# Moving two rsqrts and one DMA transpose in the opening of a two-layer attention and MLP kernel

## The chip, the cores and the metric

The kernel runs on one core of one Trainium2 chip. The metric is the device time of one execution in microseconds. The median before was 1292.16 us over three runs (1291.91 to 1292.77).

## The reference, cut to what matters

```python
x = A_x                                             # 1 x 2048 x 1024, bf16
x = x + A(layernorm(x), A_wqkv, A_wo)               # local dilated attention, 32 heads
x = x + B(layernorm(x), B_w1, B_b1, B_w2, B_b2)     # layernorm again, then a token-mixing MLP
# ... and the same two lines once more
```

Only the opening of the first attention concerns this study: load x, normalise each token, transpose it, and multiply by the V part of `A_wqkv`.

## The kernel before: the parts that the change touches

Tokens are cut into 16 tiles of 128. For each tile k the opening does this:

- SyncE (SP) loads the tile from memory (`x_load`, 256 KB).
- VectorE (DVE) forms mean and variance (`S_` twice, then `A_`).
- ScalarE (ACT) computes `R_`, the inverse root, as a Ln and an Exp of one column.
- DVE normalises the tile in place (`N_`).
- SP issues a DMA transpose into `hT` (`T_`).
- TensorE (PE) runs 16 matmuls (`V_`, 8 chunks of depth by 2 halves of the width).
- ACT evacuates the PSUM result to SBUF (`E_`), which frees its PSUM buffer.

Tiles 0 to 2 are transposed on PE instead (tiles 0 and 1 once more by DMA later, after their normalisation): PE's first V matmul starts at 6.54 us, while the first DMA transpose is issued at 14.73 us. Each engine executes its own list in order (tile 7's Ln starts at 26.13 us, behind ACT's evacuation of tile 4, though its variance was ready at 23.77 us):

```python
act = [ ..., (E_, 1), (R_, 6), (E_, 2), (E_, 3)]
rs = [(R_, k) for k in range(7, NT)]
for k in range(4, NT):            # E_4, R_7, R_8, E_5, R_9, R_10, ...
    act.append((E_, k))
    act += rs[:2]
    del rs[:2]
# dve, for each k: ..., S_(k+1, 0), N_(k), S_(k+1, 1), A_(k+1), ...
sp = [ ..., (x_load, 10), (x_load, 11), (T_, 6), (x_load, 12), (x_load, 13), (x_load, 14),
      (x_load, 15), (T_, 7), (T_, 8), (T_, 9), (T_, 0), (T_, 1), *((T_, k) for k in range(10, NT)), ...]
# V_ writes the single PSUM buffer "acc" where k % 3 == 1 (tiles 1, 4, 7, 10, 13), else one of two "s" buffers,
# so V of 6 needs the evacuation of 3, and V of 7 that of 4.
```

The softmax here doesn't subtract the row's maximum and nothing guards it: scores larger than these inputs give would overflow.

## Time and profile before

| what | value | view |
|---|---|---|
| span | 1289.9 us | page |
| PE busy | 1285.3 us | page, engines |
| PE's longest wait after its start | 0.55 us, before tile 7's V | waits of PE |
| first QK matmul | 63.73 us | timeline of PE |

The chain that ended last, from 25.2 us in the kernel before. The columns are start in us, duration in us, and what it was. L278 is the evacuation, L178 and L179 the two halves of rsqrt, L192 the normalisation, L269 the V matmuls.

```profile
25.22 1.01 ACT v L278
26.23 0.20 ACT ln L178
26.43 0.02 issue
26.46 0.21 ACT rs L179
26.67 0.03 issue
26.69 0.55 DVE x L192
27.24 0.03 DVE bn L227
27.27 5.33 DMA hT<-x
32.60 0.04 issue
32.64 3.63 PE acc L269 x16
36.27 6.91 PE s L269 x32
```

Between the first microseconds and the last instruction of the kernel, this is the only place where the chain leaves PE. Tile 7's rsqrt stands behind the evacuation of tile 4, which stands behind PE; then follow normalisation and a transpose of 5.33 us.

The timeline of PE in the same kernel. The columns are start, duration, engine, line, operation, operands, count, and the idle time just before with what ended it.

```profile
14.65 7.08 PE L269 MATMUL s<-wv,hT 128*128 128x512 bf16 x32
21.57 3.62 PE L269 MATMUL acc<-wv,hT 128*128 128x512 bf16 x16
25.02 7.07 PE L269 MATMUL s<-wv,hT 128*128 128x512 bf16 x32
32.64 3.63 PE L269 MATMUL acc<-wv,hT 128*128 128x512 bf16 x16 [0.55 <-DMA hT<-x]
36.11 7.07 PE L269 MATMUL s<-wv,hT 128*128 128x512 bf16 x32
...
63.73 0.59 PE L377 MATMUL m<-hT,wqk 128*128 128x512 bf16 x2
```

From the start of tile 2's V (14.65) to the first QK matmul (63.73) the stretch is 49.08 us. And two tiles on the `s` buffers take 6.90 to 6.92 us from start to start where nothing stalls (36.11 to 43.01 by the same view, 14.65 to 21.57), but 7.62 us where the wait lies (25.02 to 32.64), 0.71 us more than the middle of these. The idle time printed is 0.55 us. The difference of 0.16 us is an overlap that this trace shows between V groups wherever PE does not stall: the printed end of a group lies 0.16 to 0.17 us behind the start of the next (14.65 plus 7.08 is 21.73, the next starts at 21.57). Idle time counted from a printed end is short by that much here.

### The profile page before, as it was taken

How to read it: one execution, taken by the hardware profiler on the slowest of the kernel's cores; microseconds unless marked ns; L12 is line 12 of the kernel's file. 1: busy time of each engine (PE TensorE's matmuls, PEld its weight loads, DVE VectorE, ACT ScalarE, POOL GpSimd, SP SyncE). 2: the span in 40 equal slices, each digit the busy share in tenths (PEclk: the TensorE clock that was granted, in tenths of full speed). 3: DMA queues.
4: the chain of work that ended last, by engine and by line, in shares of the span. 5: the costliest groups of instructions: out<-in, count | busy, mean ns of one | idle time of the engine just before them, and what ended most of it. 6: DMA issues, size and time to landing. Idle time of an engine off the chain costs nothing.

```text
span 1289.9 us, 19532 instructions
## 1 busy us (share of the span) xinstructions
PE 1285.3 (100%) x8422; PEld 592.0 (46%) x8422; DVE 417.6 (32%) x855; ACT 369.2 (29%) x609; POOL 2.4 (0%) x15
## 2 busy tenths in 40 slices
PE   9999999999999999999999999999999999999999
PEld 4444444444444444444444444444444444444444
DVE  6566777820000022322300677688000000111111
ACT  4356664531111110000033666645311111000000
POOL 0000000000000000000000000000000000000000
PEclk9999999999999999999999999999999999999999
DMA  8711123642222144465510111247423222334330
GB/s 239 112 47 49 49 83 128 204 141 80 66 85 74 57 122 127 133 165 129 132 31 1 49 49 51 80 151 220 114 68 92 69 62 82 100 106 138 115 92 33
DMA packets 204102, 126.59 MB, mean 98 GB/s; under 512 B 44272, under 2 KB 183792, under 8 KB 204016
## 3 DMA queue, kind: packets, MB, share of 16 engines
q1 hardware_dynamic: 204016, 125.35, 34.6%
q8 instruction: 66, 1.08, 0.4%
q14 instruction: 20, 0.16, 0.0%
HBM read 96.48 MB, written 16.78 MB: 88 GB/s over the span
## 4 chain that ended last, share of the span: by engine, by line
PE 99%; DMA 1%; DVE 0%; ACT 0%; issue 0%
PE m L377 18%; PE s L619 15%; PE s L572 15%; PE m L492 9%; PE acc L619 7%; PE acc L572 7%; PE m L572 7%; PE m L619 7%; PE m L362 4%; PE s L269 2%; PE s L408 2%; PE acc L269 1%; PE acc L443 1%; PE acc L447 1%; DMA hT<-x 0%; DMA x<-in_A_x_dram 0%
## 5 line engine op out<-in xcount | busy, mean ns | idle before, releaser
L619 PEld LDWEIGHTS <-w 128*128 128x128 bf16 x1820 | 177.0, 98 | 210.1
L572 PEld LDWEIGHTS <-w 128*128 128x128 bf16 x1792 | 175.3, 98 | 211.5
L377 PE MATMUL m<-hT,wqk 128*128 128x512 bf16 x1024 | 231.7, 380 | 0.0
L572 PE MATMUL s<-h,w 128*128 128x512 bf16 x896 | 202.8, 379 | 0.0
L619 PE MATMUL s<-g,w 128*128 128x512 bf16 (+1 forms) x924 | 201.6, 374 | 0.0
L621 DVE SCALAR_TENSOR_TENSOR xo<-s,b_sb,xs 128x512 bf16<-128x512 f32 (+1 forms) x33 | 24.4, 739 | 532.9 <-PE s L619 530.8
L377 PEld LDWEIGHTS <-wqk 128*128 128x128 bf16 x1024 | 95.2, 98 | 118.0 <-issue 10.7
L423 DVE TENSOR_TENSOR Pm<-pc,band 32x640 bf16<-32x640 bf16 x256 | 123.6, 483 | 56.2 <-ACT pc L411 49.4
L492 PE MATMUL m<-wo,oT 128*128 128x512 bf16 x512 | 111.5, 379 | 0.0
L572 PE MATMUL acc<-h,w 128*128 128x512 bf16 x448 | 103.9, 379 | 0.0
L619 PE MATMUL acc<-g,w 128*128 128x512 bf16 x448 | 100.6, 379 | 0.0
L572 PE MATMUL m<-h,w 128*128 128x512 bf16 x448 | 99.0, 379 | 0.0
L619 PE MATMUL m<-g,w 128*128 128x512 bf16 (+1 forms) x448 | 97.8, 376 | 0.0
L178 ACT ACTIVATE ln<-mv,eps 128x1 f32<-128x1 f32 x64 | 18.8, 294 | 228.9 <-DVE mv L186 184.9
L492 PEld LDWEIGHTS <-oT 128*128 128x128 bf16 x512 | 49.6, 98 | 60.3 <-issue 1.3
L579 ACT ACTIVATE g<-s,b_sb 128x1024 bf16<-128x1024 f32 x28 | 31.2, 1114 | 158.2 <-PE s L572 158.2
L388 DVE COPY qB<-qs 32x512 bf16<-32x512 bf16 x136 | 38.2, 281 | 95.7 <-ACT qs L384 94.3
L362 PE MATMUL m<-wv,hT 128*128 128x512 bf16 x256 | 55.4, 379 | 0.0
L411 ACT ACTIVATE pc<-s,shift 128x640 bf16<-128x640 f32 x64 | 51.2, 800 | 11.7 <-PE s L408 11.7
L384 ACT CAST qs<-m 128x512 bf16<-128x512 f32 x64 | 37.5, 586 | 48.3 <-PE m L377 48.3
L381 ACT CAST kT<-m 128x512 bf16<-128x512 f32 x64 | 37.5, 586 | 46.4 <-PE m L377 46.4
L499 DVE TENSOR_TENSOR xn<-m,xr 128x512 bf16<-128x512 f32 x64 | 44.2, 690 | 16.9 <-PE m L492 16.8
(67 smaller groups left out, 679.7 us busy)
## 6 DMA issues: line engine op xcount, KB each, us to landing
w<-in_B_w_dram SPq DMA_DIRECT2D x56, 512.0 KB, 3.8
w<-in_B_w_dram SPq DMA_DIRECT2D x64, 448.0 KB, 4.3
wqk<-in_A_wqkv_dram SPq DMA_DIRECT2D x16, 512.0 KB, 4.9
xa<-xn SPq DMA_DIRECT2D x32, 256.0 KB, 2.2
xs<-xa SPq DMA_DIRECT2D x32, 256.0 KB, 3.0
wo<-in_A_wo_dram SPq DMA_DIRECT2D x8, 512.0 KB, 5.7
xr<-in_A_x_dram SPq DMA_DIRECT2D x16, 256.0 KB, 3.2
xb<-xo SPq DMA_DIRECT2D x16, 256.0 KB, 2.9
```

Source lines behind the costliest of these rows:

```text
L269: r = nc.tensor.matmul(pss_[k][:, n, :], lhsT=hT[:, kt, cols(*order[k])], rhs=wv[kt // 2][:, kt % 2, n * 512:(n + 1) * 512], start=(kt == ...
L362: nc.tensor.matmul(ps[:], lhsT=hT[:, kt, cols(c, i)], rhs=wv[kt // 2][:, kt % 2, n * 512:(n + 1) * 512], start=(kt == 0), stop=(kt == KD - 1))
L377: mm = nc.tensor.matmul(ps[:], lhsT=wts[part][:, kt, (g % 2) * P:(g % 2 + 1) * P], rhs=hT[:, kt, lo:lo + 512], start=(kt == 0), stop=(kt = ...
L381: nc.scalar.copy(out=kT[u % 2][:, ls], in_=ps[:])
L384: nc.scalar.copy(out=qs[:], in_=ps[:])
L388: nc.vector.tensor_copy(out=qB[u % 2][hp, h, ls], in_=qs[hp, :])
L411: nc.scalar.activation(out=pc[:].rearrange("p (n t) h k -> p n (t h k)", n=2), in_=ss[:, :, 0:2 * HG * GW], func=ACT.Exp, scale=scale, bia ...
L423: mm = nc.vector.tensor_tensor(out=Pm[rp, :, s0:s0 + HB, r * KG:r * KG + GW].rearrange("p h t k -> p t h k"), in0=pc[rp], in1=mk, op=ALU.mult)
L492: mm = nc.tensor.matmul(ps[:], lhsT=oT[g][:, cols(c, i)], rhs=wo[n][g // 4][:, g % 4, :], start=(g == 0), stop=(g == NG - 1))
L499: return nc.vector.tensor_tensor(out=xn[:, xs_], in0=pss_["o", n][:], in1=xr[:, xs_], op=ALU.add)
L572: nc.tensor.matmul(pairs[fl][0][dc], lhsT=wt[c][:, i, fl * P:(fl + 1) * P], rhs=h2[c][i][:, dc * 512:(dc + 1) * 512], start=(k == 0), stop ...
L619: nc.tensor.matmul(ap, lhsT=w2t[ft // HF][:, ft % HF, c::DIL], rhs=g[ft // GF][:, ft % GF, lo:lo + w], start=(ft == 0), stop=(ft == FT - 1))
```

## The change

Its intent is to have tile 7's transpose ready before PE asks for it. It moves tile 7's rsqrt (and tile 8's) ahead of the evacuation of tile 3, and puts tile 7's transpose between the last four token loads instead of behind them.

```diff
-               (C_, 2, 1), (R_, 4), (E_, 0), (R_, 5), (E_, 1), (R_, 6), (E_, 2), (E_, 3)]
-        rs = [(R_, k) for k in range(7, NT)]
+               (C_, 2, 1), (R_, 4), (E_, 0), (R_, 5), (E_, 1), (R_, 6), (E_, 2), (R_, 7), (R_, 8), (E_, 3)]
+        rs = [(R_, k) for k in range(9, NT)]
@@ ...
-              (x_load, 8), (x_load, 9), (T_, 5), (x_load, 10), (x_load, 11), (T_, 6), (x_load, 12), (x_load, 13), (x_load, 14),
-              (x_load, 15), (T_, 7), (T_, 8), (T_, 9), ...
+              (x_load, 8), (x_load, 9), (T_, 5), (x_load, 10), (x_load, 11), (T_, 6), (x_load, 12), (x_load, 13), (T_, 7), (x_load, 14),
+              (x_load, 15), (T_, 8), (T_, 9), ...
```

More of the change, by code (lines that the diff above doesn't have):

```diff
@@ L330, in start_up @@
               (x_load, 3), (w_load, 6), (w_load, 7), (x_load, 4), (x_load, 5), (x_load, 6), (T_, 3), (T_, 4), (x_load, 7),
-              (x_load, 8), (x_load, 9), (T_, 5), (x_load, 10), (x_load, 11), (T_, 6), (x_load, 12), (x_load, 13), (x_load, 14),
-              (x_load, 15), (T_, 7), (T_, 8), (T_, 9), (T_, 0), (T_, 1), *((T_, k) for k in range(10, NT)), (load_biases,)]
+              (x_load, 8), (x_load, 9), (T_, 5), (x_load, 10), (x_load, 11), (T_, 6), (x_load, 12), (x_load, 13), (T_, 7), (x_load, 14),
+              (x_load, 15), (T_, 8), (T_, 9), (T_, 0), (T_, 1), *((T_, k) for k in range(10, NT)), (load_biases,)]
         qs = {"PE": pe, "ACT": act, "DVE": dve, "SP": sp}
```

## The prediction

> **What bounds the kernel now.** TensorE: the page gives PE 1285.3 us busy of a 1289.9 us span, and its chain of waits is 99% PE. PE's waits in the opening (the waits view, 0 to 120 us) are 1.1 us at the very start, 0.2 us at the first transposes, and one wait of 0.55 us just before 32.64 us, "PE acc <- DMA hT<-x". After it the chain runs on PE alone until the tail. So the change can win that 0.55 us, 0.04% of the time, and nothing else.
>
> **That wait, step by step** (the chain and the timelines by engine). It is the V matmul of token tile 7, which needs the DMA transpose of tile 7. Its chain: V of tile 4 ends at 25.20; ACT, in order, evacuates tile 4 (25.22, 1.01 us) and only then does tile 7's Ln and Exp (to 26.67), though the variance was ready at 23.77; DVE normalises (26.69, 0.55 us); the transpose is issued at 27.27 behind four token loads of 256 KB (issued 24.45 to 26.53, landing at 29.58, 30.27, 30.93, 31.69) and lands at 32.60.
>
> **What the change moves.** No instruction is added or removed; PE's and POOL's orders stay the same.
> - ACT: rsqrt of 7 and 8 go ahead of the evacuation of tile 3. Rsqrt 7 runs about 23.8 to 24.3, normalise 7 about 24.35 to 24.9 (DVE's 2.4 us wait vanishes), statistics of 8 finish about 25.75, rsqrt 8 ends about 26.3.
> - SP: transpose 7 is issued about 25.5, behind two of the four loads. The two earlier transposes placed like this landed 1.06 and 1.02 us after the load ahead of them (23.69 to 24.75, 27.31 to 28.33). The load ahead now lands at 30.27, so I estimate 31.3 us, against PE ready at 32.09: 0.8 us of slack. [...]
>
> **What it costs.** Evacuation 3 waits for rsqrt 8: it ends about 27.3 instead of 22.8, evacuation 4 about 28.3 instead of 26.2. The PSUM buffer of 3 is needed by V of tile 6 at 28.47 (1.1 us slack), that of 4 by V of tile 7 at 32.1. Loads 14 and 15 land about 1.5 us later, far ahead of their statistics. Transpose 8, now behind them, should still land about 34.3 (34.33 before), needed at about 35.5. Later evacuations have a microsecond or more. All this is off the critical path.
>
> **Prediction.** 0.55 us less: 1291.6 us. Three runs before spanned 0.86 us, more than the gain, so the time alone will barely show it. Range 1290.9 to 1292.6. Faster by over 2%: 0.5%; within 2%: 99%; slower: 0.5%.
>
> **What the profile would show.** Right: no PE wait on hT near 32 us; the first QK matmul starts about 63.35 instead of 63.90 us; DVE's wait for rs near 26 us gone; span about 1289.3. Wrong in the ACT step: V of tile 6 waits for evacuation 3 near 28.4 us. Wrong in the DMA step: tile 7's V still waits, or tile 8's waits near 35.5 us for its transpose.
>
> **What would make it wrong.** The two late loads slip their packets between tile 7's, so that it lands after 32.09; transpose 8 landing over 1 us later than estimated; the token load of tile 8 (landed 23.69, needed 23.7) coming late in some executions, which now holds up evacuation 3 and so PE; a lower granted clock.

(The landing at 31.3 us is 30.27 plus the 1.06 and 1.02 us measured for the two earlier transposes, and the sum, 1292.16 less 0.55, is 1291.6 us.)

## The result, and the profile after

| | before | after |
|---|---|---|
| median of six runs | 1292.28 us | 1291.49 us |
| lowest to highest | 1291.91 to 1293.21 | 1290.93 to 1291.82 |
| span of the profiled run | 1289.9 us | 1288.8 us |

The ratio is 0.9992, with a 95% interval from 0.998 to 1.0005. Ratios here are the mean time of one kernel's fast runs over that of the other's of the same rounds, so not quite the ratio of the medians. The interval includes 1.

The timeline of PE after the change, in the same columns:

```profile
14.33 7.07 PE L269 MATMUL s<-wv,hT 128*128 128x512 bf16 x32
21.24 3.62 PE L269 MATMUL acc<-wv,hT 128*128 128x512 bf16 x15
24.69 7.07 PE L269 MATMUL s<-wv,hT 128*128 128x512 bf16 x32
31.60 3.62 PE L269 MATMUL acc<-wv,hT 128*128 128x512 bf16 x15
35.05 7.07 PE L269 MATMUL s<-wv,hT 128*128 128x512 bf16 x32
...
62.68 1.67 PE L377 MATMUL m<-hT,wqk 128*128 128x512 bf16 x7
```

The wait at tile 7 is gone: 24.69 to 31.60 is 6.91 us again. From tile 2's V to the first QK matmul it is 48.35 us, 0.73 us less than before. The remaining 0.32 us of the 1.05 us by which the first QK matmul comes sooner lie ahead of tile 2's V (14.33 against 14.65).

A caution for readers of this page. The engine line of the page after the change is:

```profile
PE 1273.3 (99%) x8266; PEld 591.8 (46%) x8422; DVE 417.6 (32%) x855; ACT 368.9 (29%) x609; POOL 2.4 (0%) x15
```

PE seems to have lost 12 us of work. It has not: 156 of the 8422 matmul records are missing from this trace (there are still 8422 weight loads), which is also why the groups above say x15 instead of x16. Starts of groups stay usable; sums do not.

ScalarE's timeline after, in the same columns, shows the moved work:

```profile
19.61 0.99 ACT L278 CAST v<-s 128x1024 bf16<-128x1024 f32 x1
23.91 0.29 ACT L178 ACTIVATE ln<-mv,eps 128x1 f32<-128x1 f32 x1 [3.31 <-DVE mv L231]
24.24 0.20 ACT L179 ACTIVATE rs<-ln 128x1 f32<-128x1 f32 x1
25.90 0.30 ACT L178 ACTIVATE ln<-mv,eps 128x1 f32<-128x1 f32 x1 [1.46 <-DVE mv L231]
26.23 0.20 ACT L179 ACTIVATE rs<-ln 128x1 f32<-128x1 f32 x1
26.34 0.99 ACT L278 CAST v<-s 128x1024 bf16<-128x1024 f32 x1
27.23 1.02 ACT L278 CAST v<-acc 128x1024 bf16<-128x1024 f32 x1
```

ScalarE now idles through two waits for statistics before evacuation 3 (the line at 26.34), which ends at 27.33; V of tile 6 starts at about 28.15 (24.69 plus 3.46 for tile 5). So 0.8 us of slack remain.

### The profile page after: what moved, and what is told of

It is laid out like the page before. It is cut to its first block, busy times and chain, and to the rows that moved or that the text cites. A ratio compares the mean times of both kernels' runs of the same rounds, so it can differ in the third digit from the quotient of the medians.

```text
span 1288.8 us, 19376 instructions
## 1 busy us (share of the span) xinstructions
PE 1273.3 (99%) x8266; PEld 591.8 (46%) x8422; DVE 417.6 (32%) x855; ACT 368.9 (29%) x609; POOL 2.4 (0%) x15
## 4 chain that ended last, share of the span: by engine, by line
PE 98%; issue 1%; DMA 0%; DVE 0%; ACT 0%
PE m L377 17%; PE s L619 15%; PE s L572 15%; PE m L492 9%; PE acc L572 7%; PE m L572 7%; PE acc L619 7%; PE m L619 7%; PE m L362 4%; PE s L269 3%; PE s L408 2%; PE acc L269 1%; PE acc L443 1%; PE acc L447 1%; DMA x<-in_A_x_dram 0%
## 5 line engine op out<-in xcount | busy, mean ns | idle before, releaser
L377 PE MATMUL m<-hT,wqk 128*128 128x512 bf16 x962 | 223.5, 379 | 6.2 <-issue 4.4
L579 ACT ACTIVATE g<-s,b_sb 128x1024 bf16<-128x1024 f32 x28 | 31.2, 1114 | 158.2 <-PE s L572 146.4
```

Of the source, the lines that this page charges most:

```text
L377: mm = nc.tensor.matmul(ps[:], lhsT=wts[part][:, kt, (g % 2) * P:(g % 2 + 1) * P], rhs=hT[:, kt, lo:lo + 512], start=(kt == 0), stop=(kt = ...
```

## The experiments

Three numbers are read from every trace: the stretch from tile 2's V to the first QK matmul, PE's printed idle time in it, and when tile 7's transpose was issued and landed, against the landing of the token load just ahead of it. From the first QK matmul to the end it took 1226.13 or 1226.14 us in all traces but those of the three kernels that changed the number of DMAs or the loads' cut (1226.18 to 1226.28), so the whole difference between spans is made before that matmul.

| run | stretch, us | PE idle | T7 issued | load ahead landed | T7 landed | later by |
|---|---|---|---|---|---|---|
| before | 49.08 | 0.55 | 27.27 | 31.69 | 32.60 | 0.91 |
| before_again | 49.10 | 0.58 | 27.32 | 31.76 | 32.67 | 0.91 |
| after | 48.35 | 0 | 25.72 | 30.22 | 31.23 | 1.01 |
| again | 48.34 | 0 | 25.55 | 30.27 | 31.26 | 0.99 |
| sp_only | 48.35 | 0 | 27.11 | 29.70 | 30.96 | 1.26 |
| rsqrt7 | 48.35 | 0 | 25.59 | 29.13 | 30.14 | 1.01 |
| t7_x14 | 48.70 | 0.17 | 26.74 | 31.18 | 32.18 | 1.00 |
| rsqrt9 | 50.12 | 1.52 | 26.54 | 29.82 | 30.84 | 1.02 |
| act_only | 50.36 | 1.71 | 27.98 | 32.60 | 34.40 | 1.80 |
| act_again | 50.20 | 1.68 | 26.83 | 31.62 | 33.42 | 1.80 |
| act7_only | 49.91 | 1.39 | 26.57 | 32.29 | 33.28 | 0.99 |
| act_whole0 | 49.23 | 0.71 | 26.07 | 31.27 | 33.02 | 1.75 |
| before_split1 | 49.64 | 1.06 | 27.93 | 32.76 | 33.75 | 0.99 |
| after_split1 | 48.35 | 0 | 26.17 | 30.71 | 31.68 | 0.97 |

All kernels of the experiments computed the right result. The edits below are shortened.

### The change once more

No edit.

> The changed kernel once more, as the control. Measure inside one trace: from the first V matmul of tile 2 to the first QK matmul (14.65 to 63.73 us before, 49.08; 14.33 to 62.68 after, 48.35). My theory (only the wait of tile 7 for its transpose was removed): again 48.35 to 48.4 us here, while the moment at which V of tile 2 begins (14.65 and 14.33 in the two traces) varies by a few tenths from run to run. Rival (the 0.33 us before 14.3 us also belong to the change): V of tile 2 begins near 14.3 in every kernel with the change, near 14.65 in every one without. Time 0.7 us under before (theory) or 1.0 us (rival).

It took 1291.21 us (five runs), the kernel before 1291.79 us; the ratio is 0.9994, interval 0.9982 to 1.0007. The stretch was 48.34 us. Tile 2's V began at 14.29 us here, which alone would favour the rival. But over all traces it began between 14.29 and 15.25 without regard to the change: 14.65 and 14.71 in the kernel before, 14.61 and 14.62 in two variants with the moved transpose, 14.36 in one without. Nor does the change move an instruction that runs before that point: the first one moved, tile 7's Ln, starts at 23.91 us. So the 0.32 us ahead of tile 2 in the result are scatter of the opening, and the change is worth 0.73 us.

### Only the ACT part

```diff
-(R_, 6), (E_, 2), (E_, 3)]            rs = [(R_, k) for k in range(7, NT)]
+(R_, 6), (E_, 2), (R_, 7), (R_, 8), (E_, 3)]   rs = [(R_, k) for k in range(9, NT)]
 # sp as before: x_load 12, 13, 14, 15, then T_ 7
```

> Only the earlier rsqrt of 7 and 8; SyncE's order as before, so the transpose of tile 7 is issued about 26.6 instead of 27.27 us, still behind all four token loads. Theory (place in the DMA queue decides): it still lands about 0.9 us after the fourth load, near 32.5, PE still waits about 0.55 us by the gap, tile 2's V to QK 49.0 us, no gain. Rival (issue time decides, landing is a fixed 5.3 us after issue): lands near 31.9, no wait left or under 0.1 us, 48.4 us.

Neither theory had it. In its trace the ACT part alone was worse than the kernel before: the stretch was 50.36 us instead of 49.08. The times agree in sign (1293.14 us against 1291.79) but do not show it, ratio 1.0008 (0.9995 to 1.002). The timeline of PE has a longer wait:

```profile
25.66 7.08 PE L269 MATMUL s<-wv,hT 128*128 128x512 bf16 x32
34.45 3.63 PE L269 MATMUL acc<-wv,hT 128*128 128x512 bf16 x16 [1.71 <-DMA hT<-x]
```

The transpose landed 1.80 us after the fourth load, not 0.91. That the issue time alone decides (a fixed 5.3 us) falls too: issue to landing took 6.4 us here.

### Only the SP part

```diff
-(x_load, 12), (x_load, 13), (x_load, 14), (x_load, 15), (T_, 7), (T_, 8)
+(x_load, 12), (x_load, 13), (T_, 7), (x_load, 14), (x_load, 15), (T_, 8)
 # act as before: E_ 2, E_ 3, E_ 4, R_ 7
```

> Only the transpose's place between the token loads; rsqrt order as before, so the transpose is still issued near 27.27 us when its normalisation ends, and loads 14 and 15 wait behind it on SyncE until about 28.5. Theory: it lands about 1.0 us after load 13, near 31.3, and the whole gain is there without the ACT part: no PE wait, 48.4 us from tile 2's V to QK. Rival (issue time decides): lands at 32.6, wait 0.55 us by the gap, 49.1 us.

The place alone brings the whole gain. SP's timeline in this run (SPq marks the issue of a DMA, not its transfer):

```profile
24.63 1.12 SPq L218 DMA_DIRECT2D x<-in_A_x_dram  x2
27.11 1.24 SPq L281 DMA_TRANSPOSE hT<-x  x1
28.39 1.43 SPq L218 DMA_DIRECT2D x<-in_A_x_dram  x2
```

The issue is as late as in the kernel before (27.11 against 27.27), yet the transpose landed at 30.96 instead of 32.60, and PE did not wait. Loads 14 and 15 were issued only after it, so its earlier place and the smaller load on the queue come together here; no run parts the two.

```profile
24.86 7.07 PE L269 MATMUL s<-wv,hT 128*128 128x512 bf16 x32
31.76 3.62 PE L269 MATMUL acc<-wv,hT 128*128 128x512 bf16 x16
```

Its time was 1291.29 us against 1291.79, the same 0.9994 as the full change. What the ACT part still buys is margin one tile later: here tile 8's transpose landed at 35.12, just ahead of its V at 35.22; in the changed kernel at 34.32, ahead of 35.05.

### One rsqrt too many

```diff
-(R_, 7), (R_, 8), (E_, 3)]
+(R_, 7), (R_, 8), (R_, 9), (E_, 3)]   rs from 10
```

> The change, with the rsqrt of tile 9 ahead of the evacuation of tile 3 as well. The evacuation of 3 must then wait for the statistics of 9 (ready 27.86 in the trace after), ends near 29.4 us instead of 27.3, and V of tile 6, due near 28.15, needs its PSUM buffer. Theory: PE waits about 1.2 us for ACT there, tile 2's V to QK 49.6 us, time about 1.2 us over the changed kernel. Rival (the scores that ACT holds up have more slack than I read): no wait, 48.4 us.

This shows the other side of the slack. PE waits for the evacuation of tile 3, as the timeline of PE has it:

```profile
25.26 3.63 PE L269 MATMUL s<-wv,hT 128*128 128x512 bf16 x16
30.41 3.61 PE L269 MATMUL s<-wv,hT 128*128 128x512 bf16 x16 [1.52 <-ACT v L278]
```

The stretch grew to 50.12 us, 0.5 us more than I expected, because tile 9's statistics came later: its Ln began at 28.93, 14.1 us after tile 2's V, where I had counted on 13.5 from the trace of the changed kernel. The time was 1292.62 us, 1.4 us over the changed kernel.

### The kernel before, and the ACT part, once more

> The kernel before once more, for the spread of its wait. Theory: the transpose of tile 7 lands 0.9 to 1.0 us after the fourth load, the gap before tile 7's V is 0.3 to 0.8 us, and tile 2's V to QK is 48.35 plus the gap plus about 0.16 us [...]. Rival, after the act_only run (where it landed 1.8 us after the load): the distance jumps between about 1.0 and 1.8 us from run to run, and this run can show either.

> The ACT part alone once more; the first time PE waited 1.71 us where the kernel before waited 0.55. If the ACT part alone really costs (the transpose of 7 now is issued right after the fourth load, that of 8 right after it[...]), tile 7's transpose again lands about 1.8 us after the fourth load, gap 1.5 to 1.9 us, tile 2's V to QK 50.2 to 50.5. If it was chance: about 0.9 us after the load, gap near 0.55, 49.1 us.

Both repeated closely: 0.91 us after the load for the kernel before, 1.80 us for the ACT part, in two traces each. Times were 1292.44 us and 1292.72 us against 1292.41 us for the kernel before. Chance from run to run is an unlikely explanation.

### The transpose after three loads

```diff
-(x_load, 13), (T_, 7), (x_load, 14), (x_load, 15)
+(x_load, 13), (x_load, 14), (T_, 7), (x_load, 15)
```

> The change, with tile 7's transpose after three of the four token loads instead of two. Theory (place in the queue, some 0.7 us per load): lands about 0.7 us later than in the changed kernel (31.25), near 31.9, just when PE needs it: gap 0 to 0.3 us, tile 2's V to QK 48.35 to 48.8. If the loads ahead did not matter: 31.25 again, no wait.

As expected, in between: landed at 32.18, PE idle 0.17 us, stretch 48.70. After two, three and four loads ahead the landings were 31.2, 32.2 and 32.6 us, each about a microsecond after the load ahead. Its time was 1292.07 us.

### Only tile 7's rsqrt moved up

```diff
-(E_, 2), (R_, 7), (R_, 8), (E_, 3)]   rs from 9
+(E_, 2), (R_, 7), (E_, 3)]            rs from 8
```

> The change, with only the rsqrt of tile 7 ahead of the evacuation of tile 3; that of 8 comes after the evacuation of 4. The evacuation of 3 ends near 25.4 us instead of 27.3, so V of tile 6 has about 2.8 us of slack instead of 0.9. Theory: the early rsqrt of 8 has no part in the gain: no PE wait, 48.35 us. Rival: tile 8's transpose is then late (normalised near 28.9, issued near 29, landing near 34.5 to 35.5) and V of tile 8, due near 35.0, waits up to 0.5 us.

The rival falls. There was no wait, and tile 8's transpose landed at 33.78, 1.5 us ahead of its V at 35.33. The time was 1291.24 us against 1292.41, ratio 0.9991 (0.9976 to 1.0006): as good as the changed kernel, with more slack on the PSUM side. It does not beat it measurably, since neither waits.

### What makes the ACT part alone worse: three attempts

In all traces one 8 KB packet of a queue that the profile calls "instruction" starts while SP issues tile 9's transpose or within 0.1 us after that (at 32.86 us in the kernel before, at 31.97 in the changed one), and the transposes' packets pause for 0.5 to 1 us, beginning 0.5 to 1.2 us later. The view of DMA between 32 and 35 us, in 40 slices of 75 ns, for the kernel before and for the ACT part alone:

```profile
GB/s 297 283 290 294 208 177 297 287 280 300 294 319 242 205 242 205 225 208 191 119 65 17 7 7 7 10 7 7 174 290 283 290 290 290 254 287 283 297 294 276
...
q14 instruction: 1, 0.01, 0.6%
```

```profile
GB/s 174 113 120 106 130 225 276 294 290 283 297 356 260 277 263 263 290 167 126 85 34 10 7 7 7 10 7 7 7 79 283 287 297 287 287 258 280 287 300 287
...
q14 instruction: 1, 0.01, 0.9%
```

Both pause, near 33.6 to 34.1 us. In the kernel before, tile 7's transpose was already through (its last packet at 31.92) and tile 8's was hit. In the ACT part alone tile 7's last packet went at 32.91, with the pause about 0.6 us after it, and it landed only at 34.40. I tried to move the packet by one DMA more or less ahead of it:

```diff
# act_whole0: the ACT part, tile 0's load as one DMA
-sp = [(x_load, 0, halves), (x_load, 1),
+sp = [(x_load, 0), (x_load, 1),
# before_split1, after_split1: the kernel before, and the changed one, with tile 1's load as two DMAs
+sp = [(x_load, 0, halves), (x_load, 1, halves),
```

> The ACT part alone with the first token load issued as one DMA instead of two halves, so that SyncE reaches every later point of its program one DMA sooner in count. In ten of ten traces one 8 KB packet of an instruction queue starts when SyncE has begun exactly 41 recorded instructions, that is in the issue of tile 9's transpose, and within about 1 us the transposes' packets pause for 0.7 to 1 us[...]. Theory [...]: the packet now comes at the next issue (tile 0's, 1.3 us later), tile 7's lands near 1 us after the fourth load, gap 0 to 0.6 us, tile 2's V to QK at most 49.1 us. Rival (two transposes issued directly behind the loads delay each other): 1.8 us after the load, gap 1.6 us, 50.2 us as before. The opening itself may be up to 1 us later, since the first half of tile 0 arrives later; that lies before V of tile 2 and is not part of the measure.

> The kernel before with the second token load issued as two halves, one DMA more ahead of everything else. Theory [...]: the 8 KB packet comes one issue sooner (in that of tile 8's transpose, 29.3 to 31.5 us) and meets tile 7's transpose, which then lands about 0.85 us later than in the kernel before: gap 1.2 to 1.6 us instead of 0.55, tile 2's V to QK about 49.9 us. Rival [...]: 49.1 us, gap 0.55.

> The changed kernel with the second token load issued as two halves. Theory [...]: the packet now comes in the issue of tile 8's transpose (28.2 to 30.4 us) while tile 7's is in flight (packets 28.3 to 30.65); it lands up to 0.85 us later, 31.9 to 32.1 instead of 31.2, where PE needs it at about 31.5: gap 0.2 to 0.6 us, tile 2's V to QK 48.5 to 49.1. Rival: 31.2, no wait, 48.35 us.

The edit did not move the packet: in all three it still came in, or just behind, the issue of tile 9's transpose, so the count of DMAs does not set it and the manipulation failed. act_whole0 again landed 1.75 us after the load (its shorter stretch comes from PE having started later against the loads: the fourth landed 16.3 us after tile 2's V began, in act_only and act_again 17.4 and 17.3). before_split1 waited 1.06 us, but with a normal 0.99 us after the load; there the loads themselves were later against PE (the fourth landed 17.5 us after tile 2's V began, in the kernel before 17.0). after_split1 did not wait. Times were 1292.5, 1292.82 and 1291.96 us, of two runs each, against 1291.38 us for the kernel before (three runs); none of the ratios is clear of 1.

One attempt was left. The ACT part alone issues tile 8's transpose 1.35 us after tile 7's; the kernel before 2.0 us after. So I moved up only tile 7's rsqrt:

```diff
# act7_only: sp as before
-(E_, 2), (E_, 3)]            rs from 7
+(E_, 2), (R_, 7), (E_, 3)]   rs from 8
```

> SyncE's order as before, and only the rsqrt of tile 7 ahead of the evacuation of tile 3; that of 8 after the evacuation of 4, so that tile 8's transpose is issued near 29 us, over 2 us after tile 7's (26.6 to 27), as it is in the kernel before (2.0 us) and not as in the ACT part alone (1.35 us, three traces, each with tile 7's transpose landing 1.75 to 1.8 us after the fourth load). If the close following of tile 8's transpose brings the late landing: about 0.9 to 1.0 us after the load again, gap near 0.5 us, tile 2's V to QK 49.1 us or less. If the early issue of tile 7's transpose brings it: 1.8 us after the load, gap 1.6 us, 50.2 us.

The edit did not part the two, because tile 8's transpose was again issued 1.34 us after tile 7's (27.91 against 26.57): my estimate of 29 us for it was wrong. Yet both suspects were there, and the transpose landed 0.99 us after the load: by the measure set beforehand, neither is enough to make it late. PE waited all the same, 1.39 us, because that load itself landed 0.6 to 0.7 us later than in the kernel before or act_again, at nearly the same issue (26.05 us). The call ran on a chip of which there is no trace of the kernel before, so what made the load late stays open. The time was 1294.06 us against 1292.76; the traced run was the quickest of the four (1292.63).

From the issue of the fourth load to the landing of tile 7's transpose it took 7.0 to 7.5 us in the four ACT-only traces, against 6.5 and 6.7 in the two traces of the kernel before and 6.3 in before_split1. This measure was chosen after the results, and it mixes the late load of act7_only with a late landing in the other three. The packets kept in the traces part them (a transpose is 1024 packets of 256 bytes). In all seven traces tile 7's last packet started 0.2 to 0.3 us after the fourth load had landed. From there to its landing it took 0.67 to 0.75 us in the kernel before, before_split1 and act7_only, but 1.50 to 1.55 us in act_only, act_again and act_whole0. In just these three the 8 KB instruction packet had started within 0.1 us of tile 7's last packet. In the two traces of the kernel before and in before_split1 it fell so on tile 8's last packet, and there tile 8's landing took 1.45 to 1.46 us. No other transpose of tiles 7 to 9 whose landing the 14 traces give took more than 0.75 us.

So the late landing goes with the instruction packet meeting the last packet of a transpose. It does not go with the sooner issue as such (before_split1 also issued tile 7's transpose 0.5 us after the load), nor with tile 8's following closely (act7_only). No run moved that packet alone: that it causes the delay, and why it falls where it does, is not shown.

## Why the prediction was right, point by point

- **What bounds it, and the only wait.** Right. The stretch after the first QK matmul did not change by more than 0.01 us in any trace of the two kernels.
- **The size of the wait.** Undersized. I took the printed idle time, 0.55 us; start to start, the wait cost 0.71 to 0.73 us, since the printed end of the matmul before it hides 0.16 us. Of the 0.79 us between the medians the change explains 0.73; the opening's scatter can hold the rest, and runs this noisy do not resolve it. That the median came within 0.11 us of the 1291.6 predicted is therefore partly luck, and the range of 1.7 us, wider than the gain, would have held an unchanged kernel too (1292.28); what bears the prediction out is the trace.
- **ACT and DVE steps.** Right: rsqrt 7 ended at 24.44 (predicted 24.3), rsqrt 8 at 26.43 (26.3), evacuation 3 at 27.33 (27.3), evacuation 4 at 28.25 (28.3), the transpose was issued at 25.72 (25.5).
- **The landing.** Right: 31.23 us against an estimated 31.3. The rule used, about 1 us after the load ahead, held where loads followed the transpose (0.97 to 1.26 us in seven traces). In sp_only, too, a late issue behind fewer loads landed early (30.96 us instead of 32.60). It is not the whole of it: in three of the four ACT-only traces the order of the kernel before gave landings up to 0.9 us later (1.75 to 1.80 us after the load instead of 0.91).
- **Which part earns it.** The prediction presented both moves as steps of one gain. The runs separate them: the place between the loads is enough, the earlier rsqrt is not needed for the gain, and without the other move every trace of it had a longer wait than the kernel before (0.71 to 1.71 us against 0.55 and 0.58).
- **The costs.** Right in kind. The slack of evacuation 3 was 0.8 us instead of 1.1, and rsqrt9 shows that it is real: one more rsqrt cost 1.77 us of stretch. Tile 8's transpose landed at 34.32 as estimated (34.3).
- **First QK matmul at 63.35, span 1289.3.** Missed by 0.67 and 0.5 us (62.68 and 1288.8). The 63.90 that I started from is the chain's figure, which lies 0.17 us behind the record's start (63.73); another 0.18 us is the undersized wait, and 0.32 us the opening's scatter.

## What to carry to other kernels

Ask what stands in the DMA queue ahead of the transfer that the critical engine waits for; here moving it ahead of two bulk loads gained 0.73 us (sp_only), while issuing it sooner behind them left PE waiting 0.71 to 1.71 us. Cost a TensorE stall by the distance between starts of matmul groups (0.71 us here), not by the idle time printed (0.55). When a change worth less than the scatter of the times is judged, find a stretch inside the trace that only the change can alter, and repeat the trace before believing a side effect.

Watch the issues of a series of DMA transposes too. In the kernel before, the four 256 KB loads 12 to 15 landed 0.66 to 0.76 us apart, while the transposes of tiles 0, 1, 10 and 11, of the same size and with no other data in the queue, landed 1.24 to 1.49 us apart, with SP spending 1.24 to 1.32 us on each issue and starting one every 1.33 to 1.50 us. Two that were already queued (8 and 9, in the changed kernel) landed 0.84 us apart.
